# Batch 3's strided crossbar transposes two steps sooner, and the last strided P·v of batch 0 behind its local ones

## The chip, the core and the metric

The kernel runs on one core of a Trainium2 chip. Five engines work side by side, each through its own queue in order: PE (matmuls), DVE and ACT (element-wise work), POOL (which here mostly issues loads) and SP (which here issues stores and the crossbar transposes). They meet only at semaphores. The metric is the device time of one execution in microseconds, and for a kernel the median over its runs.

## What is computed

Sparse attention over eight batches, followed by a feed-forward layer. Cut to what matters:

```
q, k, v: 8 batches x 8 heads x 576 positions x 64
heads 0-3: keep keys with 0 <= i-j < 32                 (local)
heads 4-7: keep keys with i >= j and i%32 == j%32       (strided)
x   = softmax(q k^T / 8, masked) v  ->  4608 x 512
h   = x @ w_in                      (512 x 2048)
out = elu(h) @ w_out                (2048 x 512)
```

## The kernel before

**Attention.** A batch has four head pairs: `hp` 0 and 1 are local, 2 and 3 strided. Each pair has two halves `u`, so a batch has eight pieces, numbered 0 to 7 as `P[n]` (0 to 3 local, 4 to 7 strided). For a piece, `S` (`piece_S`) makes the scores on PE (L290), their exponential on ACT (L293) and the masked product `pm` on DVE (L295 or L301). `M` (`mm_O2`) multiplies `pm` with ones and with v on PE, `E` (`tail_O2`) takes the logarithm and the reciprocal on ACT (L382, L384), and one DVE product (L310 or L314) writes the piece into `xT`, the transposed x. `X` is `M` and `E` together; from batch 3 on `O` (`piece_O`, L342 to L348) does the same job with wider matmuls.

**q and k transposed.** S needs q and k with the head dimension on the partitions. Batches 0 and 1 transpose on PE (L267, L536). From batch 2 on `dma_T` issues four crossbar transposes from SP's queue (L164): `qs` and `ks` for the strided heads into `qsT` and `ksT`, `kl` and `ql` for the local heads. The tiles `qs` and `ks` are single, so a batch's strided q can be loaded only when the transpose of the batch before has read it. `vs`, the strided v of batches 0 to 2, is single too. `vl32` holds batch 0's local v in f32; `cast_v` turns its halves into `vlx`, half 0 on DVE and half 1 on POOL (L153).

**Feed-forward.** `l1(j, t)` (L403) makes 256 tokens times 256 of the 2048 hidden columns with eight matmuls, ACT and DVE apply elu into `g`; `l1_wide` (L428) makes 512 columns at once. `l2` (L460) is a quarter of the second product for 128 tokens, four matmuls; after the fourth quarter ACT copies the sum to `osb` (L465) and SP stores it (L448). Hidden quarter `part` needs `w_out_sb` loaded by `load_wo(part)`.

**Order.** All of it is written out by hand, for every queue at once: an engine does its part of each item in program order. Batch 0 is the list of L522: `f7` puts seven idle matmuls (L484) on PE, `T1` a transpose, `m` the mask, `v` the two casts, `S4`, `M4`, `E4` the pieces above. After it POOL issues, in this order, the loads `qs`, `ks` of batch 1, `w_out` quarters 0 and 1, `vs` of batch 1, `w_out` quarters 2 and 3, and then batch 1's local q, k and v. Then come two token groups with wide first products, batch 1 in a second list, and the main loop over `L1S`, whose step `n` is one call of `l1`. The lists `jobs[n]` run ahead of step n's `l2` calls, `jobs[n + .5]` behind them and ahead of its `l1`. Batch 2's scores are at `SC[2]`, its X 1.5 steps later and each u half a step later; batch 3's strided scores are at step 15, its local ones from step 23 on, and its four transposes at step 12. On POOL every load also waits for the eighth load before it, since there are eight completion semaphores.

Of the kernel before, what the change touches and what calls it, by code (L numbers as in the profile page):

```python
# [30 lines left out]
def kernel(  # L31
# [34 lines left out]
    def const(shape, dt, name):  # L66
        return consts.tile(shape, dt, tag=name, name=name)
# [6 lines left out]
    qs = const([RP, HG, NS * D], BF16, "qs")  # L74
    ks = const([RP, HG, NS * D], BF16, "ks")
# [36 lines left out]
    def load_ql16(b):  # L112
        for h in range(HG):
            nc.gpsimd.dma_start(  # L114
                out=qlb[b % 2][0:RS, h // 2, :, (h % 2) * D:(h % 2 + 1) * D],
                in_=q[b, h].rearrange("(p s) d -> p s d", s=NS))

    def load_kl16(b):
        for h in range(HG):
            nc.gpsimd.dma_start(  # L120
                out=klb[b % 2][:, h // 2, :, (h % 2) * D:(h % 2 + 1) * D],
                in_=k[b, h].rearrange("(t p) d -> p t d", p=LQ))

    def load_vl16(b):
        for h in range(HG):
            x = v[b, h].rearrange("(t p) d -> p t d", p=LQ)
            t = vlx[b % 2][:, h // 2, :, 2 * (h % 2) * D:(2 * (h % 2) + 1) * D]
            nc.gpsimd.dma_start(out=t[PRE:128], in_=x)  # L128
            nc.gpsimd.dma_start(out=t[0:PRE, 1:], in_=x[LQ - PRE:, 0:LB - 1, :])  # L129

    def load_vsx16(b):
        for h in range(HG):
            nc.gpsimd.dma_start(  # L133
                out=vsx[b % 2][:, h // 2, :, 2 * (h % 2) * D:(2 * (h % 2) + 1) * D],
                in_=v[b, HG + h].rearrange("(p s) d -> p s d", s=NS))

    def load_str(b, dst, src):
        nc.gpsimd.dma_start(  # L138
            out=dst[0:RS], in_=src[b, HG:2 * HG].rearrange("h (p s) d -> p h (s d)", s=NS))
# [11 lines left out]
    def cast_v(eng, b, a):  # L151
        o = vlx[b % 2][:, a].rearrange("p t (y d) -> p t y d", d=D)[:, :, 0:3:2, :]
        (eng.copy if eng is nc.scalar else eng.tensor_copy)(  # L153
            o, vl32[:, a].rearrange("p x t d -> p t x d"))

    def dma_T(b, which):
        i = b % 2
        out_, in_, n = {
            "qs": (qsT[i], qs.rearrange("p h c -> p (h c)"), RP),
            "ks": (ksT[i][:, 0:16 * RP], ks.rearrange("p h c -> p (h c)"), RP),  # L160
            "ql": (qlT[i], qlb[i].rearrange("p a s c -> p (a s c)"), RP),
            "kl": (klT[i][:, PRE:], klb[i].rearrange("p a t c -> p (a t c)"), LQ),
        }[which]
        nc.sync.dma_start_transpose(out=out_.rearrange("p (c n) -> p c n", n=n), in_=in_)  # L164
# [59 lines left out]
    def mask_strided():  # L224
        same = p_wk.tile([RS, RS], I32, tag="he1", name="same")
        eq = p_wk.tile([RS, RS], BF16, tag="he1", name="eq")
        nc.vector.tensor_scalar(same, dist, scalar1=STRIDE // NS - 1, scalar2=None,
                                op0=ALU.bitwise_and)
        nc.vector.tensor_scalar(eq, same, scalar1=0, scalar2=None, op0=ALU.is_equal)
        nc.vector.scalar_tensor_tensor(mask_s, dist, float(RS), eq, op0=ALU.is_ge,  # L230
                                       op1=ALU.mult)
# [7 lines left out]
    def t_parts(b, hp, nm):  # L239
        i, a, n = b % 2, hp % 2, RS  # L240
        if hp >= 2:
            src = qs if nm == "q" else ks
            dst = (qsT if nm == "q" else ksT)[i][:, a * 8 * n:(a + 1) * 8 * n]
            blk = [src[0:n, 2 * a + j // 4, (j % 4) * 128:(j % 4 + 1) * 128] for j in range(8)]
        elif nm == "q":
            dst = qlT[i][:, a * 8 * n:(a + 1) * 8 * n]
            blk = [qlb[i][0:n, a, j] for j in range(NS)]
        else:
            dst = klT[i][:, PRE + a * S:PRE + (a + 1) * S]
            blk = [klb[i][:, a, j] for j in range(LB)]  # L250
        return dst, blk

    def copy(eng, dst, src):
        (eng.copy if eng is nc.scalar else eng.tensor_copy)(dst, src)

    def piece_T(b, hp, engs=None, wide=True):
        both = [t_parts(b, hp, nm) for nm in "qk"]
        if wide:
            pw = p_x.tile([128, 2, 1024], BF16, tag="x", name="tp2")
            ps = [pw[:, 0, 0:S], pw[:, 1, 0:S]]  # L260
        else:
            ps = [p_h.tile([128, S], BF16, tag="h", name="tp") for _ in range(2)]
        for i, (dst, blk) in enumerate(both):
            n = S // len(blk)
            for j, x in enumerate(blk):
                o = ps[i][:, j * n:(j + 1) * n]
                nc.tensor.transpose(o, x, identity[0:n, 0:n])  # L267
        for i, (dst, blk) in enumerate(both):
            copy(engs[i] if engs else nc.vector, dst, ps[i])
# [219 lines left out]
    def do(it):  # L489
        kind = it[0]  # L490
        if kind == "TT":
            piece_T(*it[1:])
        elif kind == "S":
            pms[it[1:4]] = piece_S(*it[1:])
        elif kind == "SS":
            for u in range(2):
                pms[(*it[1:3], u)] = piece_S(*it[1:3], u)
        elif kind == "O":
            piece_O(*it[1:4], pms.pop(it[1:4]))
        elif kind == "M":  # L500
            sos[it[1:4]] = mm_O2(*it[1:4], pms.pop(it[1:4]), it[4])
        elif kind == "E":
            tail_O2(*it[1:4], sos.pop(it[1:4]))
        elif kind == "X":
            tail_O2(*it[1:4], mm_O2(*it[1:4], pms.pop(it[1:4]), p_x))
# [4 lines left out]
    def spins(n):  # L510
        for _ in range(n):
            spin(idle)
# [6 lines left out]
    cast_q(nc.vector, 1)  # L519
    cast_k(nc.vector, 1)  # L520
    P = [(p, u) for p in range(4) for u in range(2)]
    for it in ("f7 S0 S1 f6 T1 f6 S2 S3 m f8 T2 T3q T3k f3 S4 S5 f3 S6 S7 M4 f3 E4 M5 f3 E5 M6 f3 E6 "  # L522
               "v M7 f3 E7 M0 f3 E0 M1 f3 E1 M2 f3 E2 M3 f12 E3").split():
        n = int(it[1:].strip("qk")) if len(it) > 1 else 0
        if it == "m":
            mask_strided()
        elif it[0] == "f":
            spins(n)
        elif it == "v":
            cast_v(nc.vector, 0, 0)  # L530
            cast_v(nc.gpsimd, 0, 1)
        elif it[0] == "T" and len(it) == 3:
            dst, blk = t_parts(0, n, it[2])
            ps = p_h.tile([128, S], BF16, tag="h", name="tp")
            for j, x in enumerate(blk):
                nc.tensor.transpose(ps[:, j * RS:(j + 1) * RS], x, identity[0:RS, 0:RS])  # L536
            copy(nc.vector, dst, ps)
        elif it[0] == "T":
            piece_T(0, n, (nc.vector, nc.scalar if n > 1 else nc.vector), False)
        elif it[0] == "S":  # L540
            do(("S", 0, *P[n]))
        elif it[0] == "M":
            do(("M", 0, *P[n], p_h))
        else:
            do(("E", 0, *P[n]))
# [41 lines left out]
    def Ts(b, *names):  # L587
        for w in names:
            dma_T(b, w)
# [30 lines left out]
    def at(n, *its):  # L620
        jobs.setdefault(int(2 * n) / 2, []).extend(its)


    SC = {2: (4.5, 7.5, 10, 12.5), }
    SC.update({b: tuple(15 + 16 * (b - 3) + 4 * i for i in range(4)) for b in range(3, B)})

    for b in range(3, B):
        st = int(SC[b][0])
        if b > 3:
            at(st - 13, lambda b=b: (load_str(b, qs, q), load_str(b, ks, k), load_kl16(b),  # L630
                                     load_ql16(b), load_vsx16(b), load_vl16(b)))
        at(st - (3 if b == 3 else 4), lambda b=b: Ts(b, "qs", "ks", "kl", "ql"))
    for b in range(2, B):
        for i, p in enumerate((2, 3, 0, 1)):
            for u in range(2):
                at(SC[b][i] + (.5 * u if b == 2 else 0), lambda b=b, p=p, u=u: do(("S", b, p, u)))
                at(SC[b][i] + 1.5 + .5 * u,
                   lambda b=b, p=p, u=u: do(("X" if b == 2 else "O", b, p, u)))
# [40 lines left out]
```

The softmax here doesn't subtract the row's maximum and nothing guards it: scores larger than these inputs give would overflow.

## Time and profile before

| | |
|---|---|
| median of 13 runs | 323.45 us (320.28 to 325.65) |
| the profiled execution | 320.28 us, its span 318.6 us |
| PE busy | 304.8 us (96%) |
| DVE, ACT busy | 237.8 us, 219.5 us |
| POOL busy | 121.0 us |
| granted TensorE clock | 1.00 throughout |
| chain that ended last | PE 82%, DMA 8%, DVE 5%, ACT 3% |

The profiled execution is the shortest of the 13. The span runs from the first to the last instruction; 1.7 us of the time lie around it. The chain follows the last instruction back to what released it, step by step, so a transfer on it is a transfer that PE stood or would have stood for. A wait is put down to whatever was seen to come last.

### The profile page before, as it was taken

The page shows a single profiled execution, that of the slowest core. Times are in us where ns is not written, and L with a number is a line of the kernel's source. Part 1 is how long each engine was busy: PE and PEld are TensorE (multiplying, and loading weights), DVE is VectorE, ACT ScalarE, POOL GpSimd, SP SyncE. Part 2 cuts the span into 40 slices and gives each one's busy share as a digit, 9 for nine tenths or more (in the row PEclk, how much of TensorE's full clock was granted, in tenths as well). Part 3 has the DMA queues.
Part 4 walks back from the last instruction along what each step waited for, and adds up shares of the span by engine and source line. Part 5 has one row for each costly group of instructions (what it writes and reads, how often), then busy time and mean ns, then how long its engine had stood idle before and what let it go on. Part 6 is the DMA issues. An engine that isn't in the chain of part 4 may idle for free.

```text
span 318.6 us, 7608 instructions
## 1 busy us (share of the span) xinstructions
PE 304.8 (96%) x2857; PEld 221.7 (70%) x2900; DVE 237.8 (75%) x478; ACT 219.5 (69%) x428; POOL 121.0 (38%) x168
## 2 busy tenths in 40 slices
PE   8899999889989999999999999999999999999995
PEld 6659945566657777777777777777777777777764
DVE  7665975376668888888888888888888866666660
ACT  7486766677878777778778877777788644443431
POOL 6352469476967904780559057700000000000000
PEclk9999999999999999999999999999999999999999
DMA  7999999999999949994999599929111111112112
GB/s 167 189 204 208 211 132 122 177 170 180 156 182 190 126 76 142 193 127 53 136 163 166 85 140 203 122 60 168 37 33 35 36 33 33 36 34 51 48 33 69
DMA packets 124583, 37.66 MB, mean 118 GB/s; under 512 B 112322, under 2 KB 118050, under 8 KB 124546
## 3 DMA queue, kind: packets, MB, share of 16 engines
q0 software_dynamic: 85168, 18.87, 63.4%
q1 hardware_dynamic: 37886, 17.56, 28.2%
q10 hardware_dynamic: 1492, 0.74, 0.9%
q8 instruction: 23, 0.38, 0.5%
q14 instruction: 14, 0.11, 0.1%
HBM read 38.04 MB, written 9.44 MB: 149 GB/s over the span
## 4 chain that ended last, share of the span: by engine, by line
PE 82%; DMA 8%; DVE 5%; ACT 3%; issue 2%; DVEq 0%; ACTq 0%
PE ops L460 35%; PE hps L403 34%; DMA ksT<-ks 5%; PE sc L290 3%; PE ox L342 3%; DMA kl<-in_k_dram 2%; PE idle L484 2%; DVE g L418 1%; DVE g L437 1%; PE hpw L428 1%; PE opl L475 1%; DVE he L417 1%; ACT big L434 1%; PE o_ps L375 1%; PE tp L267 1%
## 5 line engine op out<-in xcount | busy, mean ns | idle before, releaser
L403 PE MATMUL hps<-xT,w_in_sb 128*128 128x256 bf16 x1088 | 140.6, 273 | 0.7 <-DVE xT L314 0.4
L460 PE MATMUL ops<-w_out_sb,g 128*128 128x512 bf16 x517 | 137.1, 380 | 2.5 <-issue 0.6
L403 PEld LDWEIGHTS <-w_in_sb 128*128 128x128 bf16 x1088 | 117.4, 114 | 22.8 <-issue 0.8
L410 ACT ACTIVATE he<-hps 128x512 f32<-128x512 f32 x136 | 80.3, 593 | 53.3 <-PE hps L403 52.9
L418 DVE TENSOR_TENSOR g<-he,hps 128x512 bf16<-128x512 bf16 x130 | 89.4, 688 | 13.9 <-PE hps L403 0.5
L460 PEld LDWEIGHTS <-g 128*128 128x128 bf16 x560 | 50.5, 98 | 37.2 <-DVE g L418 0.3
L417 DVE TENSOR_SCALAR he<-he 128x512 bf16<-128x512 f32 x130 | 58.1, 447 | 20.8 <-ACT he L410 19.4
L293 ACT ACTIVATE e<-sc 128x576 bf16<-128x576 f32 (+1 forms) x64 | 38.7, 647 | 6.6 <-PE sc L290 6.6
L114 POOL DMA_DIRECT2D qlb<-in_q_dram x28 | 23.2, 833 | 17.1 <-DMA ks<-in_k_dram 9.0
L465 ACT COPY osb<-ops 128x512 f32<-128x512 f32 x35 | 20.6, 588 | 9.9 <-PE ops L460 7.1
L120 POOL DMA_DIRECT2D klb<-in_k_dram x28 | 21.2, 766 | 10.2 <-DMA w_in_sb<-in_moe_w_in_dram 5.8
L345 ACT ACTIVATE ln<-ox 64x288 f32<-64x288 f32 x40 | 16.4, 409 | 10.5 <-PE ox L342 10.0
L128 POOL DMA_DIRECT2D vlx<-in_v_dram x28 | 22.0, 785 | 2.5 <-DMA qlb<-in_q_dram 1.1
L314 DVE TENSOR_TENSOR xT<-ox,rc 64x288 bf16<-64x288 f32 x40 | 18.1, 453 | 5.8 <-ACT rc L348 5.5
L310 DVE TENSOR_TENSOR xT<-ox,rc 64x288 bf16<-64x288 f32 x40 | 18.1, 454 | 4.8 <-ACT rc L348 4.6
L138 POOL DMA_DIRECT2D qs<-in_q_dram x8 | 6.2, 771 | 34.5 <-DMA qsT<-qs 32.7
L348 ACT ACTIVATE rc<-ln 128x288 f32<-128x288 f32 x40 | 17.7, 443 | 1.3
L129 POOL DMA_DIRECT2D vlx<-in_v_dram x28 | 17.7, 633 | 1.7 <-DMA klb<-in_k_dram 0.9
L133 POOL DMA_DIRECT2D vsx<-in_v_dram x20 | 16.2, 818 | 1.9 <-PE hps L403 1.2
L346 ACT ACTIVATE ln<-ox 64x288 f32<-64x288 f32 x40 | 16.1, 403 | 0.5
L301 DVE TENSOR_TENSOR pm<-e,mask_l 128x576 bf16<-128x576 bf16 x32 | 13.6, 453 | 3.7 <-ACT e L293 3.4
L295 DVE TENSOR_TENSOR pm<-e,mask_s 72x576 bf16<-72x576 bf16 x32 | 13.6, 450 | 3.3 <-ACT e L293 2.9
(98 smaller groups left out, 232.9 us busy)
## 6 DMA issues: line engine op xcount, KB each, us to landing
out_dram<-osb SPq DMA_DIRECT2D x31, 144.0 KB
qs<-in_q_dram POOLq DMA_DIRECT2D x8, 288.0 KB, 6.8
ks<-in_k_dram POOLq DMA_DIRECT2D x8, 288.0 KB, 8.2
w_in_sb<-in_moe_w_in_dram POOLq DMA_DIRECT2D x2, 1024.0 KB, 17.6
w_out_sb<-in_moe_w_out_dram POOLq DMA_DIRECT2D x4, 512.0 KB, 15.8
klb<-in_k_dram POOLq DMA_DIRECT2D x28, 72.0 KB, 7.7
qlb<-in_q_dram POOLq DMA_DIRECT2D x28, 72.0 KB, 6.4
vlx<-in_v_dram POOLq DMA_DIRECT2D x28, 72.0 KB, 3.6
```

The costliest lines, as they stand in the source:

```text
L114: nc.gpsimd.dma_start(out=qlb[b % 2][0:RS, h // 2, :, (h % 2) * D:(h % 2 + 1) * D], in_=q[b, h].rearrange("(p s) d -> p s d", s=NS))
L120: nc.gpsimd.dma_start(out=klb[b % 2][:, h // 2, :, (h % 2) * D:(h % 2 + 1) * D], in_=k[b, h].rearrange("(t p) d -> p t d", p=LQ))
L128: nc.gpsimd.dma_start(out=t[PRE:128], in_=x)
L293: nc.scalar.activation(e[0:R], sc[0:R, :, 0:W], ACT.Exp, scale=scale)
L310: nc.vector.tensor_mul(xs[:, u * W:(u + 1) * W], o[pr], rc[pr])
L314: nc.vector.tensor_mul(dst, o[pr].rearrange(pat, b=3, s=NS), rc[pr].rearrange(pat, b=3, s=NS))
L403: nc.tensor.matmul(hps[:, mm], lhsT=w_in_of(m, c), rhs=xT[:, c, r0:r0 + SUB], start=(c == 0), stop=(c == KC - 1))
L410: nc.scalar.activation(e, hps, ACT.Exp)
L417: eng.tensor_scalar(e1, e, scalar1=1.0, scalar2=1.0, op0=ALU.min, op1=ALU.subtract)
L418: nc.vector.tensor_tensor(gt, e1, hps, op=ALU.max)
L460: nc.tensor.matmul(ops, lhsT=g[:, m, kk * 128:(kk + 1) * 128], rhs=w_out_sb[:, m, :], start=(m == 0), stop=(m == MC - 1))
L465: nc.scalar.copy(o_sb, ops)
```

## The change

Three edits.

- In batch 0 the item `M7 E7` (the last strided piece) moves from ahead of the local pieces to behind them. The casts `v` move from behind E6 to ahead of M6. Five idle matmuls stand where M7 stood, and the twelve ahead of E3 become three ahead of E3 and three ahead of E7.
- Batch 2's first strided scores move from step 4.5 to 5. Its second half and the two X that follow move half a step with them.
- Batch 3's crossbar transposes are split: `qs` and `ks` at step 10 instead of 12, `kl` and `ql` at step 13 instead of 12. For later batches all four stay four steps ahead.

```diff
-    for it in ("... S6 S7 M4 f3 E4 M5 f3 E5 M6 f3 E6 "
-               "v M7 f3 E7 M0 f3 E0 M1 f3 E1 M2 f3 E2 M3 f12 E3").split():
+    for it in ("... S6 S7 M4 f3 E4 M5 f3 E5 v M6 f3 E6 f5 "
+               "M0 f3 E0 M1 f3 E1 M2 f3 E2 M3 f3 E3 M7 f3 E7").split():
...
-    SC = {2: (4.5, 7.5, 10, 12.5), }
+    SC = {2: (5, 7.5, 10, 12.5), }
...
-        at(st - (3 if b == 3 else 4), lambda b=b: Ts(b, "qs", "ks", "kl", "ql"))
+        at(st - (5 if b == 3 else 4), lambda b=b: Ts(b, "qs", "ks"))
+        at(st - (2 if b == 3 else 4), lambda b=b: Ts(b, "kl", "ql"))
```

On SP's queue this moves batch 3's `qs` and `ks` transposes ahead of one store (two transfers, L448); the local ones stay behind it. On POOL's queue nothing changes place, but the load of `vs` for batch 1 may start only when M7 has read the old `vs`.

## The prediction

> **What bounds the kernel now.** I read the chain that ended last first, in order of time (start, length, what):
>
> ```profile
> 23.67 1.42 PE idle L484 x12
> 25.09 1.76 PE hpw L428 x16
> ...
> 57.70 9.37 DMA ksT<-ks
> 67.07 0.05 issue
> 67.11 0.30 PE sc L290 x8
> ...
> 85.15 7.11 DMA ksT<-ks
> 92.26 0.05 issue
> 92.31 0.43 PE sc L290 x16
> ```
>
> PE carries 82% of the chain, and from 92.3 us on the chain is matmuls nearly without a break. What can be won lies ahead of that: the end of batch 0, where idle matmuls hold the place until E3 is done, and two crossbar transposes of `ks`, for batch 2 (landing at 67.07) and batch 3 (at 92.26). Being on the chain for 9.37 and 7.11 us says only that PE met their end. How long PE stood is in PE's waits, between 50 and 100 us:
>
> ```profile
> PE sc L290 <- DMA ksT<-ks: 1.5, 2, 1.2
> PE so L365 <- DVE pm L295: 0.7, 1, 0.7
> ```
>
> So the transposes cost 1.54 us in two waits: the timeline gives 0.30 at 67.11 and 1.24 at 92.31. The 0.7 stands at 70.72, where batch 2's second X waits for its masked product. Next the loads, which decide how early a transpose can start. POOL's timeline (start, length, and in brackets the idle time before it and what ended it):
>
> ```profile
> 19.60 0.82 POOL L153 CAST vlx<-vl 128x768 bf16<-128x768 f32 x1 [8.97 <-DMA vl<-in_v_dram]
> ...
> 22.94 0.75 POOL L138 DMA_DIRECT2D vs<-in_v_dram  x1
> ...
> 43.83 0.81 POOL L114 DMA_DIRECT2D qlb<-in_q_dram  x1 [1.77 <-DMA w_out_sb<-in_moe_w_out_dram]
> ...
> 77.61 0.73 POOL L120 DMA_DIRECT2D klb<-in_k_dram  x1 [1.21 <-DMA qs<-in_q_dram]
> ...
> 79.59 0.73 POOL L120 DMA_DIRECT2D klb<-in_k_dram  x1 [1.25 <-DMA ks<-in_k_dram]
> ```
>
> POOL's wait for the eighth load before dates the landings: local v of batch 0 just before 19.60, the last `w_out` quarter by 43.83, batch 3's strided q by 77.61 and k by 79.59. SP's timeline has what came of the last two:
>
> ```profile
> 81.22 1.18 SPq L448 DMA_DIRECT2D out_dram<-osb  x2
> 82.57 2.47 SPq L164 DMA_TRANSPOSE qsT<-qs  x1
> 85.15 2.26 SPq L164 DMA_TRANSPOSE ksT<-ks  x1
> 87.64 2.89 SPq L164 DMA_TRANSPOSE klT<-klb  x1
> ```
>
> Data that was there at 77.61 was taken up at 82.57, because a store that waits for ACT's copy (80.59 + 0.61) stands ahead on SP.
>
> **Batch 3's strided transposes at step 10.** They pass one store, and SP has been free since about 72.4. qsT goes with its load at 77.6, ksT one spacing later (85.15 - 82.57 = 2.58), at 80.2, when `ks` has landed too. From issue to landing ksT took 7.11 us here and 9.37 in batch 2: it lands at 87.3 to 89.6. PE asks for it at 92.31 - 1.24 = 91.07, or some 0.35 sooner by the edits below, 90.7. The slack is 1.1 to 3.4 us, so the whole 1.24 goes. Bounds: all 1.24, or nothing if, beside POOL's loads, the transpose took 12 us. The passed store leaves SP at 82.5 instead of 81.2; ACT's next copies come at 89.73 and 99.48 and there are three buffers, so nobody waits. The local transposes come behind that store. klT cannot go before the last `klb` load, issued at 79.59 with a median of 7.7 us to landing: 87.3, as now (87.64). Step 13 is no later than the data; PE uses them at 108.20. Batch 4's strided loads wait for these transposes to read `qs`; POOL is busy to 89.9, so they gain under 3 us, and need nothing.
>
> The Trainium skill ("DMA: Bandwidth & Descriptors", Queues, rings and completion order) speaks against this edit: each DMA engine takes turns between the queues that have work, packet by packet, so a transpose put among POOL's loads shares with them. By that rule alone, with 7.11 us taken for the undisturbed length, ksT takes up to twice that, lands at 94.4, and the sum is -0.3 instead of the -1.55 that the rows give. The row is already in such company: the DMA share was 1.73 from 67 to 91 us, and 7.11 and 9.37 are its lengths there; at 118.29, with little else, the next ksT landed in about 6 (POOL resumed at 124.48).
>
> **Batch 2's scores half a step later.** l1 of step 4 (1.01 us) then runs ahead of the scores, and ksT is there: the 0.30 goes. Both halves now follow each other, and the first X waits instead of the second. The chain prices that: from the end of l1(4) at 68.43 to the product ready for PE at 70.72 are 2.29 us (elu on ACT and DVE, then `pm`). Beside them PE has two S (0.24 each), l1(5) (1.00): 1.48, so it stands 0.8 us. Before it stood 0.7. Net -0.2. Bounds: -1.0 if DVE takes `pm` ahead of that elu product (0.69), +0.5 if the second X, now behind l1(6), delays the next scores' PSUM buffer.
>
> **Batch 0.** Half 0 of the cast ran 20.00 to 20.83 on DVE, behind E6's product; its data was there at 19.60. Moved ahead it ends at 19.60 + 0.83 = 20.43, 0.4 sooner, and M0 to M3 with it (M0 stood 0.52 for it). M3 then ends at 23.67 - 0.41 = 23.26, E3's product at 24.92 - 0.41 = 24.51; in between PE has three idle matmuls (0.43), M7 (0.37) and three more (0.43), to 24.49. So the wide product starts at 24.51 instead of 25.09: -0.58. M7 covers E3 for nothing; E6's product is late by 0.8 but no one asks for it before 24.5. The first wide product reads `xT` only up to token 256, E7 writes from 288 on, and its DVE product (about 25.4) is far ahead of the second group at 28.3. Bounds for the cast: the same width of k took DVE 0.56 alone (L147), and this one 0.83 with 0.42 us beside POOL's 0.82. If they share, it ends at 20.15; if DVE waits for POOL's to end, at 20.42 + 0.56 = 20.98. That makes the stage -0.58 - 0.28 to 0.
>
> The skill ("SBUF — State Buffer", Who interferes with whom) has copies and casts on DVE and anything on POOL contend for one port pair, held for a whole instruction, when DVE's form takes both ports. If it applies, the later of the casts is served last, and this stage's gain shrinks to nothing: a sum of -1.45 instead of -1.55.
>
> But the 0.58 does not arrive. At 42.73 PE begins the third and fourth l2 quarter of the first tile, the fourth at about 43.70, and the load of that quarter was noted by POOL at 43.83 after waiting 1.77. PE cannot be earlier than a load that landed just there, and the loads stand in one queue that moves with nothing on PE. I let 0.1 through, between 0 and 0.58.
>
> M7's move has a price on POOL: `vs` of batch 1 went out at 22.94, now it waits for M7 to 24.1, and `w_out` quarters 2 and 3 and `klb` behind it. Cover: POOL stood at 24.8 anyhow until 30.54 for `w_in` to land, so the load queue was full; the price is 0, or 1.2 if it ran dry.
>
> **The sum.** -0.1 - 0.2 - 1.24 = -1.55 us on the profiled execution: 318.7 against 320.28. It was the shortest of 13, 3.2 us under the median. PE's work is fixed (clock 1.00), so I take that excess for loads landing later, spread over the six places where PE came within a microsecond of one (19.6, 24.8, 43.7, 67.1, 91.1 and the start). One sixth, 0.5, then adds to the wait at 91.1, which the edit covers. -2.1 on the median: 321.3.
>
> **The rivals.**
>
> *The waits in a median run are longer.* For it: the spread of 5.4 us with matmuls that never vary. If two thirds of the 3.2 us stand at the two ksT waits, the gain is 1.55 + 2.1 = 3.7: 319.8. Chance 0.16.
>
> *The transpose lands no sooner.* Put among the loads of `klb` and `qlb` it takes 12 us, or the waits fall to the next load. Then only batch 2's part and the 0.1 stay: 323.1. Against it: 9.37 is the longest seen. Chance 0.24.
>
> *The load queue, not SP, sets the pace.* M7 at the end holds `vs` and two `w_out` quarters for 1.2 us. If POOL's queue has run dry by then, quarter 3 lands at 45.0, PE's l2 waits from 43.7, all loads behind it slip too, and `ks` of batch 3 with them, so step 10 finds no data. It decides if `ks` lands later than 82.4, when the old order on SP would have been ready as well. Price 1.2 to 2, each way nothing gained: 324.6 to 325.5. Against it: 5.8 us of POOL's standing behind a full queue. Chance 0.18.
>
> **How the numbers follow.** My forecast, 321.3 with its own range 320.0 to 322.4, has 0.42. About 0.5% (1.6 us, the line at 321.8 and 325.1) is what a measurement of this kernel can tell from no change. Faster: 0.35 of my forecast, all 0.16 of the longer waits, 0.03 of the second rival: 0.54. Slower: 0.12 of the third rival. The same: the rest, 0.34. The range reaches from the better rival to the milder half of the slower one: 319.0 to 324.3, leaving out about 0.2.
>
> **What would show it.** Right: PE's wait for ksT gone at both places, qsT issued near 77.6 and before the store, the wide product at 24.5, and at 43.7 a new short wait for `w_out`. PE's wait for `pm` stays near 0.8 and now at the first X. Wrong: ksT(3) landing after 90; the fourth `w_out` quarter later than 44; a span that keeps its length with all these waits gone, which would mean ACT or DVE takes their place.

## The result, and the profile after

The changed kernel has a median of **319.32 us** (318.86 to 320.14, 11 runs), beside 323.32 us (319.89 to 325.69, 48 runs) for the kernel before: a ratio of 0.990, 95% interval 0.9874 to 0.9926. Ratios and intervals, here and below, leave out executions more than 1.5% above the fastest of their kernel (nine of the 48 here); by the two medians, which are of all runs, the ratio would be 0.988. The forecast was 321.3 with a range of 319.0 to 324.3. The direction was right; the median lies 2 us beyond it, below the forecast's own range (320.0 to 322.4) and next to the first rival's 319.8.

The two profiled executions hardly show this: 320.14 us (span 318.4) after, 320.28 (span 318.6) before. The profile of before was of one of its shortest executions, that of after of the longest of its eleven. So "after" against "before" in these two traces is short against long, and the 4 us must be looked for in other executions. First, though, the rows that the prediction named. The chain that ended last of after, in order of time (start, length, what):

```profile
25.92 17.60 DMA w_out_sb<-in_moe_w_out_dram
43.53 0.04 issue
43.57 1.02 PE ops L460 x4
...
80.67 10.74 DMA ksT<-ks
91.41 0.05 issue
91.46 0.43 PE sc L290 x16
```

Batch 3's scores begin at 91.46 instead of 92.31, and the chain now passes through the last `w_out` quarter, where it used to pass through the idle matmuls of batch 0. The transpose was issued 4.5 us sooner (80.67 for 85.15), but took 10.74 us instead of 7.11. SP's timeline of after shows it ahead of the store, as the edit says:

```profile
78.52 1.91 SPq L164 DMA_TRANSPOSE qsT<-qs  x1
80.67 4.11 SPq L164 DMA_TRANSPOSE ksT<-ks  x1
84.89 1.26 SPq L448 DMA_DIRECT2D out_dram<-osb  x2
90.33 1.38 SPq L164 DMA_TRANSPOSE klT<-klb  x1
```

PE's waits of after between 50 and 100 us (engine, line, waited for: us in total, times, the longest) still have the transposes in them:

```profile
PE sc L290 <- DMA ksT<-ks: 1.3, 2, 0.7
PE so L365 <- DVE pm L295: 0.4, 1, 0.4
```

Now the kernel before, profiled once more (`before_again` below): 323.12 us, close to its median. The same view of that execution:

```profile
PE sc L290 <- DMA ksT<-ks: 3.6, 2, 2.4
PE so L365 <- DVE pm L295: 0.7, 1, 0.7
```

3.6 us instead of the 1.54 on which the prediction's sum was built, in the same two places.

### The profile page after: what moved, and what is told of

The parts are those of the page before. It is cut to its first block, busy times and chain, and to the rows that moved or that the text cites. A ratio compares the mean times of both kernels' runs of the same rounds, so it can differ in the third digit from the quotient of the medians.

```text
span 318.4 us, 7602 instructions
## 1 busy us (share of the span) xinstructions
PE 304.1 (95%) x2853; PEld 221.1 (69%) x2896; DVE 239.1 (75%) x478; ACT 219.5 (69%) x428; POOL 120.8 (38%) x168
## 4 chain that ended last, share of the span: by engine, by line
PE 76%; DMA 12%; ACT 4%; DVE 4%; issue 2%; POOL 1%; DVEq 0%; ACTq 0%
PE ops L460 34%; PE hps L403 33%; DMA w_out_sb<-in_moe_w_out_dram 6%; DMA ksT<-ks 3%; PE ox L342 3%; PE sc L290 3%; DMA ks<-in_k_dram 3%; PE opl L475 1%; ACT rc L384 1%; DVE he L417 1%; ACT ln L382 1%; DVE xT L310 1%; DVE g L418 1%; ACT e L293 1%; PE tp L267 1%
## 5 line engine op out<-in xcount | busy, mean ns | idle before, releaser
L403 PE MATMUL hps<-xT,w_in_sb 128*128 128x256 bf16 x1088 | 140.6, 273 | 0.7 <-DVE xT L314 0.4
L403 PEld LDWEIGHTS <-w_in_sb 128*128 128x128 bf16 x1088 | 117.5, 114 | 23.0 <-issue 0.8
L417 DVE TENSOR_SCALAR he<-he 128x512 bf16<-128x512 f32 x130 | 59.2, 455 | 20.4 <-ACT he L410 18.9
L345 ACT ACTIVATE ln<-ox 64x288 f32<-64x288 f32 x40 | 16.4, 409 | 10.8 <-PE ox L342 10.3
L314 DVE TENSOR_TENSOR xT<-ox,rc 64x288 bf16<-64x288 f32 x40 | 18.1, 453 | 5.6 <-ACT rc L348 5.3
```

Source lines behind the costliest of these rows:

```text
L314: nc.vector.tensor_mul(dst, o[pr].rearrange(pat, b=3, s=NS), rc[pr].rearrange(pat, b=3, s=NS))
L403: nc.tensor.matmul(hps[:, mm], lhsT=w_in_of(m, c), rhs=xT[:, c, r0:r0 + SUB], start=(c == 0), stop=(c == KC - 1))
L417: eng.tensor_scalar(e1, e, scalar1=1.0, scalar2=1.0, op0=ALU.min, op1=ALU.subtract)
```

## The experiments

Three theories of where the 4 us of the medians come from. *Waits*: in most executions of the kernel before, the two waits for `ksT` are longer than in its profile, and the change covers them. *List*: batch 0's new order is worth far more than the 0.1 us let through. *Spread*: the excess is shared by many waits, and no edit is worth much by itself. Each run was timed beside the kernel before on the same chip; the medians of that were 323.89, 323.58 and 323.43 us in the three sessions. "S(b)" is the first strided score of batch b on PE.

**The kernel before once more** (no edit, one profiled execution).

> The kernel before once more, for a second profile of it. The first profile was of an execution 3 us below the median. If the excess of the median stands at batch 3's strided transpose (theory 1), an execution near 323 us shows PE waiting 3 to 5 us for ksT at the scores of step 15, with ksT landing at 94 to 96 us. If it stands at batch 0 or at the w_out loads (theory 2), PE's waits for ksT stay under 2 us and the wide products or the l2 quarters at 43 us begin 1 to 3 us later than in the first profile.

Measured: 323.12 us. The wait for `ksT` is 1.17 at S(2) and 2.39 at S(3), which starts at 94.80; the row of the latter stands beside others further down. The landing is where theory 1 had it, the wait at S(3) is shorter than its 3 to 5 us, and the 1.17 at S(2) stood in neither theory.

**Each edit alone.** The three kernels are the kernel before with one hunk each:

```diff
 only_transposes
-        at(st - (3 if b == 3 else 4), lambda b=b: Ts(b, "qs", "ks", "kl", "ql"))
+        at(st - (5 if b == 3 else 4), lambda b=b: Ts(b, "qs", "ks"))
+        at(st - (2 if b == 3 else 4), lambda b=b: Ts(b, "kl", "ql"))
 only_list
-    "... v M7 f3 E7 M0 f3 E0 ... M3 f12 E3"
+    "... v M6 f3 E6 f5 M0 f3 E0 ... M3 f3 E3 M7 f3 E7"
 only_scores
-    SC = {2: (4.5, 7.5, 10, 12.5), }
+    SC = {2: (5, 7.5, 10, 12.5), }
```

> Only the third edit: batch 3's strided transposes at step 10, its local ones at step 13. Theory 1: nearly all of the gain, 2.5 to 3.7 us under before, about 320, and the spread of single runs shrinks to about 1.5 us. Theory 2 (the list of batch 0 pays): within 1 us of before. Theory 3 (batch 2's scores half a step later pay): within 1 us of before.

> Only the first edit: M7 behind the local pieces, the casts ahead of M6. Theory 1: 0 to 0.3 us under before, the spread of before (about 5 us) kept. Theory 2: 2 us or more under before.

> Only the second edit: batch 2's scores half a step later. Theory 1: 0 to 0.4 us under before, the spread kept; the saved wait of 0.3 us for ksT comes back as a wait of 0.8 us for pm at the first X instead of 0.7 at the second. Theory 3: 1 us or more under before, since ksT of batch 2 lands late in most runs.

| alone | median us (runs) | ratio, 95% interval | S(3) starts, wait for ksT |
|---|---|---|---|
| transposes | 321.53 (10) | 0.9937, 0.9907 to 0.9968 | 92.96, none |
| list | 322.58 (12) | 0.9961, 0.9926 to 0.9996 | 94.14, 1.62 |
| scores | 323.24 (12) | 0.9976, 0.9945 to 1.0008 | 94.08, 2.88 |

Only the transposes remove S(3)'s wait. PE's timeline of `only_transposes`:

```profile
92.96 0.30 PE L290 MATMUL sc<-qsT,ksT 64*128 64x72 bf16 x8
```

The second score then waits 0.35 us for its PSUM buffer, which DVE's product into `xT` (L314) frees; that is the next limit there. The list makes the wide product earlier, and the wait that the prediction named appears; PE's timeline of `only_list` (start, length, and in brackets the idle time before it):

```profile
44.02 1.02 PE L460 MATMUL ops<-w_out_sb,g 128*128 128x512 bf16 x4 [0.92 <-DMA w_out_sb<-in_moe_w_out_dram]
```

The scores lose their wait for `ksT` at S(2), gain 1.13 at the first X, and S(3) waits longer for it: beyond what the interval can tell. By the medians the three gain 2.4, 1.3 and 0.65 us. The transposes thus stay just under their 2.5 to 3.7, with a spread of 3.0 us where 1.5 was expected, and the other two lie between their theories (0 to 0.3 or 2, and 0 to 0.4 or 1).

**Each edit undone**, the other two kept, with the changed kernel again.

```diff
 no_transposes                                    (hunk 3 undone)
-        at(st - (5 if b == 3 else 4), lambda b=b: Ts(b, "qs", "ks"))
-        at(st - (2 if b == 3 else 4), lambda b=b: Ts(b, "kl", "ql"))
+        at(st - (3 if b == 3 else 4), lambda b=b: Ts(b, "qs", "ks", "kl", "ql"))
 no_list                                          (hunk 1 undone)
 no_scores                                        (hunk 2 undone)
```

> The changed kernel once more, as the measure for the three kernels beside it: 319 to 320 us, 1% or more under before, single runs within 1.5 us of each other. Its second profile tells whether the waits left at ksT (0.61 and 0.67 us in the first) stand there each time.

> The change without its third edit: all four transposes of batch 3 at step 12, the first two edits kept. If the edits take away separate waits (theory A), it loses what the third edit won alone, 2.0 to 2.6 us against the changed kernel, and single runs spread over 4 us or more; PE waits 2 to 4 us for ksT at step 15, more than before, since PE comes there earlier and the loads do not. If the gains overlap (theory B, the load queue sets the time once), it loses under 1 us.

> The change without its first edit: batch 0's list as before, the other two kept. Theory A: 0.3 to 1.3 us slower than the changed kernel, all of it before 45 us, as batch 1's first P v on PE begins that much later. Theory B: within 0.3 us of it.

> The change without its second edit: batch 2's first scores at step 4.5, the other two kept. Theory A: 0.4 to 1.0 us slower than the changed kernel, with PE waiting 1.0 to 1.7 us for ksT at batch 2's scores. Theory B: within 0.3 us, the time lost at batch 2 being won back at ksT of batch 3.

| | median us (runs) | ratio, 95% interval |
|---|---|---|
| changed kernel | 320.10 (6) | 0.9896, 0.9858 to 0.9933 |
| transposes undone | 322.89 (12) | 0.9977, 0.9946 to 1.0007 |
| list undone | 320.10 (6) | 0.9897, 0.9857 to 0.9937 |
| scores undone | 321.28 (12) | 0.9942, 0.9907 to 0.9978 |

The transposes are worth 2.8 us with the others in place and 2.4 alone. The scores are worth 1.2 with the transposes early and 0.65 alone, the list nothing when undone and 1.3 alone. An interval of one ratio reaches some 1.0 to 1.3 us each way, so only the first is settled; with the transposes undone nothing measurable is left of the change. Against the expectations, the transposes lose a little more than theory A's 2.0 to 2.6 (with the wait of 3.01 it had), the list follows theory B, and without the scores' edit PE waits 0.93 at S(2), a little less than theory A's 1.0 to 1.7. The second profile of the changed kernel has no wait for `ksT` at all, and its runs spread over 2.0 us instead of 1.5.

**Is it the store, or the local transposes' absence?** The edit does two things: the strided transposes pass a store, and the local two no longer follow them at once.

```diff
-        at(st - (2 if b == 3 else 4), lambda b=b: Ts(b, "kl", "ql"))
+        at(st - (5 if b == 3 else 4), lambda b=b: Ts(b, "kl", "ql"))
```

> The change with the local transposes at step 10 too, so that all four stand ahead of the store. If passing the store is what pays (theory S), it is within 0.3 us of the changed kernel: qsT goes at 77 to 79 us as there, klT is issued when its load lands at 85 to 90, the store is held until qlT is out, near 92, and no copy of ACT waits for a buffer. If keeping the local transposes away pays (theory K, fewer transposes in flight behind ksT), PE waits 1 us or more longer for ksT and the kernel is 1 to 2 us slower.

Measured: 319.63 us (6 runs; 0.987, 0.9826 to 0.9913), the changed kernel beside it 319.16 (`after_third`, 6 runs; 0.987, 0.9821 to 0.9919). S(3) starts at 90.58 without a wait. The kernel is 0.47 us above the changed one, more than the 0.3 of theory S but less than six runs can tell; the longer wait of theory K is not there. So passing the store is what pays; that the local transposes go to step 13 has no effect that these runs can show.

> The changed kernel a third time, as the measure for the three beside it: about 1.0% under before.

**Two attempts to go further.** One puts batch 3's strided scores half a step later, behind one more `l2`, to take away the 0.35 us for the PSUM buffer; one issues the two late `w_out` quarters ahead of `vs`, so that POOL does not hold them until M7 has read it.

```diff
 scores3_later
+    SC[3] = (15.5, 19, 23, 27)
 w_out_first
-    load_wo(1); load_str(1, vs, v); load_wo(2); load_wo(3)
+    load_wo(1); load_wo(2); load_wo(3); load_str(1, vs, v)
```

> The change with batch 3's strided scores half a step later too (step 15.5, so that an l2 of four matmuls, 0.97 us, runs ahead of them; the two O follow half a step later). Theory A (PE's waits at the strided scores are what is left): the wait for ksT, 0 to 0.7 us, and the 0.35 us for the PSUM buffer go, 0.3 to 0.8 us under the changed kernel. If the masked product or the reciprocal comes late in their place, no change.

> The change with the loads of w_out quarters 2 and 3 issued ahead of batch 1's vs, so that M7 at the end of batch 0 holds back vs alone. If the last w_out quarter is what takes batch 0's 0.5 us away (as forecast), quarter 3 lands 1 to 2 us sooner, PE shows no wait for it and begins batch 1's first P v 0.2 to 0.5 us sooner than the changed kernel. If the load queue sets the pace further on, ksT of batch 2 lands when it did, PE stands there 0.2 to 0.5 us longer or the slack of the later scores takes it, and the time is that of the changed kernel within 0.5 us.

Measured: 319.46 us (6 runs; 0.9871, 0.9825 to 0.9918) and 319.99 (6 runs; 0.9885, 0.9837 to 0.9934). The first does remove the 0.35, S(3) starts at 91.87 with neither wait, and the 0.3 to 0.8 us expected do not come; six runs could not have shown 0.3. The second does what it was to do: the wait for `w_out` is gone and PE's first P·v of batch 1 starts at 44.30 (mean of the other eight traces with the new list: 44.66). But batch 2's `ksT` is then issued at 59.74 (56.95 to 59.03 in those eight), and S(2) waits 2.40 us. The loads stand in one queue, and in this execution, one of the two longest of its six, what is gained at 44 us is lost at 69. Neither beats the changed kernel.

**The clock.** One thing was in the results that no theory had asked for. Each execution is recorded with its mean granted TensorE clock. Of 59 executions of the kernel before, counted as for the ratios, 21 had 0.997 or more, with a mean of 322.39 us; 38 had 0.995 or less, with a mean of 324.36. The 24 executions recorded of the changed kernel all had 0.998 or more. Over all kernels, 53 of 92 executions with batch 3's `ksT` at step 12 had 0.995 or less, and 7 of 70 with it at step 10. Three profiles fell on such an execution, and each shows where the clock went. In `no_transposes`, PE's timeline has the longest wait for `ksT` of all traces:

```profile
94.73 0.43 PE L290 MATMUL sc<-qsT,ksT 64*128 64x72 bf16 x16 [3.01 <-DMA ksT<-ks]
```

The same execution by stretches, cut at that wait (columns: stretch; its length; busy time and instructions of PE, PEld, DVE, ACT and POOL; granted clock; DMA share; GB/s):

```profile
91.70:94.73 3.03, 0.02 (x2) 0.01 (x2) 1.57 (x3) 0.65 (x2) 2.06 (x3) 1.00 1.53 201
94.73:96.00 1.27, 1.11 (x19) 0.72 (x21) 0.25 (x1) 0.93 (x2) 0.73 (x2) 0.96 1.83 215
96.00:97.70 1.70, 1.70 (x9) 1.22 (x8) 0.66 (x2) 0.26 (x1) 1.70 (x3) 0.50 1.12 194
97.70:99.38 1.68, 1.68 (x7) 0.61 (x4) 0.29 (x1) 1.08 (x2) 1.68 (x3) 0.52 1.10 161
99.38:100.60 1.22, 1.22 (x20) 1.21 (x19) 0.40 (x1) 0.75 (x2) 1.22 (x3) 1.00 1.36 222
```

PE stands still, resumes at full clock, and about a microsecond later runs at half clock for some 3.4 us. The loss is (1.27 x 0.04) + (1.70 x 0.50) + (1.68 x 0.48) = 1.71 us. In `only_scores` (wait 2.88 at 94.08) the same sum gives 1.71, in `w_out_first` (wait 2.40, at batch 2) 1.70. The row of that shortest wait, from PE's timeline, and the two stretches behind it:

```profile
69.58 0.43 PE L290 MATMUL sc<-qsT,ksT 64*128 64x72 bf16 x16 [2.40 <-DMA ksT<-ks]
69.58:70.50 0.92, 0.92 (x21) 0.84 (x22) 0.00 (x0) 0.57 (x2) 0.78 (x2) 0.93 2.22 167
70.50:71.50 1.00, 1.00 (x7) 0.46 (x7) 0.81 (x2) 0.61 (x2) 0.63 (x2) 0.50 1.35 126
```

The matmuls show it too: eight of L403 take 1.04 us in all otherwise, and in `only_scores` behind the wait

```profile
94.08 0.43 PE L290 MATMUL sc<-qsT,ksT 64*128 64x72 bf16 x16 [2.88 <-DMA ksT<-ks]
94.67 1.13 PE L460 MATMUL ops<-w_out_sb,g 128*128 128x512 bf16 x3 [0.16 <-issue]
95.59 1.91 PE L403 MATMUL hps<-xT,w_in_sb 128*128 128x256 bf16 x8
```

The span keeps the loss: from S(3) to the end are 228.2 and 228.6 us in `no_transposes` and `only_scores`, and 226.3 to 227.6 in the other traces with the scores at step 15, which keep full clock from there on. A wait of this length is not always followed by it. In `before_again`, PE's timeline

```profile
94.80 0.43 PE L290 MATMUL sc<-qsT,ksT 64*128 64x72 bf16 x16 [2.39 <-DMA ksT<-ks]
```

and the clock stays at 1.00. The Trainium skill ("TensorE: Matmul & The Clock Gate", Part 1) says that a monitor looks at PE's activity in windows of 3413 ns that run freely, and halves the clock after an idle window. The half clock and the length of the stretch agree with that: 1.71 us lost at half clock are 3.42 us of it. Its rule of thumb on that page, no idle gaps above about 3.4 us ("HAM oscillation — how this bites in real kernels"), does not: 2.40 us was enough here once, and 2.39 was not another time. Nor can a window of 3.4 us be idle throughout in a wait of 2.40. If each fall of the clock is taken as the end of a window, PE was idle for some 2.2, 2.5 and 2.4 us of the 3.42 ahead of it (`no_transposes`, `only_scores`, `w_out_first`; an estimate from the stretches). Free-running windows that need not be idle throughout would then explain that the same wait is punished in one execution and not in the next, by whether it falls into one window or is split over two; no run here tests it, as none shortens the wait alone without moving work.

## Why the prediction was right, and where its size was off

**The strided transposes: the mechanism right, the term too small.** The store stood in the way, and passing it pays. Of the sum's 1.24 (1.74 with the share of the median's excess) the experiments make 2.4 to 2.8 us. What failed is the step "I take that excess for loads landing later, spread over the six places ... One sixth, 0.5". Where most of the excess of 3.2 us of the median over the profiled execution lies can be estimated from the traces:

- at S(2) and S(3): the two waits for `ksT` were 1.54 us in all in the profile used, and 3.56, 3.10, 2.88 and 3.01 in the four later traces with the transposes at step 12 (`before_again`, `only_list`, `only_scores`, `no_transposes`): on average 1.6 more. They are added up by execution, since where S(2) does not wait S(3) waits longer;
- the clock: 38 of 59 executions lose the 2.0 us between the two groups, 1.3 on average.

Together 2.9; it is no exact account, as two of the four traces are of other kernels' longest or nearly longest executions. Without the clock's part, `before_again` is 2.8 us longer than the first profile, both at clock 1.00, and 2.0 of these stand at the two waits. The excess was not spread over six places: about half of it or more stands at the two waits that the change shortens (the first rival had two thirds, 2.1), and much of the rest is not waiting at all but the clock behind a long wait. That rival had 0.16; "the spread of 5.4 us with matmuls that never vary" was named for it and given too little weight. The matmuls do vary: "PE's work is fixed (clock 1.00)" holds in the execution that was profiled and not in the 38 of 59. That the result still lies in the stated range of 319.0 to 324.3 is owed to the rival's end of that range, not to the sum.

**The landing.** "It lands at 87.3 to 89.6" was too early; in the profile after it landed at 91.4, and 0.67 us of wait stayed. In the other seven traces with step 10 and the scores at step 15 S(3) did not wait for it, starting at 90.02 to 93.24. Issue to PE's start was 10.8 us in the profile after and 7.2 to 8.9 in the five traces of step 12. The Trainium skill's rule that the prediction weighed ("DMA: Bandwidth & Descriptors", Queues, rings and completion order: an engine takes turns between queues that have work) agrees in its direction: of 4.5 us of earlier issue, 3.6 went back in the profile after. That sharing is the reason was not tested; the DMA share of the two stretches was 1.91 and 1.79. The length did not double, so the edit kept its gain. "9.37 is the longest seen", said against the second rival, held for the first profile alone: batch 2's `ksT` took 11.4 us in `only_transposes`. The test named in the prediction, a landing after 90, came true without the conclusion drawn from it, since PE asked for the data at 90.8.

**Batch 2's scores.** Forecast -0.2: 0.30 less for `ksT`, 0.1 more at X. The exchange of waits is there (0.76 to 1.13 at the first X in the traces with a wait for `pm` there, 0.40 in the profile after), but the wait for `ksT` that it covers is about 1.2 us, not 0.30. Measured 0.65 alone and 1.2 undone, neither settled by itself. The term was mis-sized by the same step. It may also keep the clock: without it (`no_scores`) 4 of 12 executions had a lowered clock, with all three edits (`after`, `after_again`, `after_third`) none of 24. That is not settled, for with the transposes alone (`only_transposes`, old scores too) it was none of 10, and in `scores3_later`, which has all three edits, 1 of 6.

**Batch 0's list, up to the wide product.** On average the stage gains what the working had (0.58): in PE's timeline the wide product starts at 24.4 in nine traces with the new list and at 25.0 in five with the old. But the working failed at the cast, and the mean agrees only because the data usually comes sooner than in the profile of before. POOL's and DVE's timelines of after:

```profile
19.34 0.82 POOL L153 CAST vlx<-vl 128x768 bf16<-128x768 f32 x1 [8.63 <-DMA vl<-in_v_dram]
```

```profile
19.40 1.18 DVE L153 CAST vlx<-vl 128x768 bf16<-128x768 f32 x1
```

Begun 0.06 after POOL's, DVE's cast ends 0.42 after it (20.58 against 20.16). It ends 0.41 to 0.42 after POOL's in all eight traces where it began while POOL's ran, however much it had already run (0.72 to 1.18 long); alone it takes 0.55. In `scores3_later` DVE was first by 0.02, and it was POOL that waited:

```profile
19.37 0.55 DVE L153 CAST vlx<-vl 128x768 bf16<-128x768 f32 x1
```

```profile
19.39 1.22 POOL L153 CAST vlx<-vl 128x768 bf16<-128x768 f32 x1 [8.35 <-DMA vl<-in_v_dram]
```

So the later one stands for nearly all of the earlier one's length, and only some 0.13 us of it run beside (0.55 - 0.42; in `scores3_later`, where POOL's ends at 20.61 and DVE's at 19.92, 0.82 - 0.69). "Moved ahead it ends at 19.60 + 0.83 = 20.43" took the 0.83 for the cast's own length, while its end hung on POOL's: 20.42 + 0.41 = 20.83, where it already was. The Trainium skill's rule of the shared port pair ("SBUF — State Buffer", Who interferes with whom), which the prediction quoted against this term, agrees with these rows but for the 0.13, and for a landing at 19.60 it takes all that the moved cast was to bring. The gain follows the landing: with v there at about 19.35 the wide product starts 0.29 sooner (24.63 in after, 24.92 in `no_list`), with v there at 18.77 to 18.94 0.8 sooner (mean of four 24.22, of three with the old list 25.05), for then the old list's cast stood behind E6's product and the new one's does not.

**Batch 0's list, behind it.** "I let 0.1 through" is the weaker point. The first P·v of batch 1 starts at 44.66 instead of 45.22 us on average, so some 0.55 arrives, although the wait for `w_out` of 0.9 to 1.0 appears in some traces (44.02 above) as announced; the prediction's sign of being wrong, that quarter later than 44, came true in `no_transposes`, where the wait ended at 44.63. What it is worth in the end stays open: 1.3 us alone, nothing when undone.

**The rivals that failed.** Transposes that land no sooner: excluded by S(3) and by `all_four_at_10`. A load queue that sets the pace: `vs` went out at 24.65 after 1.94 us of waiting for M7, much as forecast (24.1), the last `w_out` quarter was noted by POOL at 43.7 us on average with the new list and 43.2 with the old, and `qs` of batch 3 was there by 78.5. The loads slip by half a microsecond on average and not by 1.2 to 2. The local transposes and the store went later than forecast in the profile after (klT at 90.33 for 87.3, the store at 84.89 for 82.5), but klT was used near 107, and nobody waited for either.

## What to carry to other kernels

When the profiled execution is one of the shortest of a wide spread, size an edit by a second profile near the median: here the two waits were 1.5 us in the one and 3.6 in the other. Read the granted clock of all executions, not only of the profiled one, for a wait of 2.4 us or more on TensorE can cost another 1.7 us behind it, and an edit that shortens it gains both and the spread with it. In a queue written by hand, look for a transfer whose data has landed and which stands behind a store that waits for another engine; moving it ahead can pay even when the transfer then takes longer.

## What the runs showed of the hardware

- Behind PE's waits of 2.40, 2.88 and 3.01 us the granted clock fell to 0.50 about a microsecond after PE had resumed, and came back 3.4 us later, a loss of 1.7 us each time; behind 2.39 us in another execution it did not fall.
- The same crossbar transpose of `ks` took 7.2 to 8.9 us from issue to PE's start when issued for batch 3 at 85 to 87 us, 10.8 when issued at 80.67 (DMA share 1.91, and 1.77 to 1.89 in the five), and at most 5.8 for batch 4, where little else was on its way (118.29, used without a wait at 124.05 in the profile of before).
- Casts from f32 to bf16 on DVE and POOL at once were served nearly in turn: DVE's, 0.55 us alone, ended 0.41 to 0.42 us after POOL's in eight traces, wherever it had begun.
